# Retention and softmax-gated MLP on one core: from tile 20 the activation is transposed by DMA, with three more load buffers and new orders

## The chip, the cores and the metric

The kernel runs on one core of a Trainium2 chip. The core has a matrix engine (TensorE; PE in the tables, with PEld for its weight loads), a vector engine (DVE), a scalar engine (ACT), a general engine (POOL), and a queue engine (SP) that issues DMAs; all five run their own instruction lists and wait for each other by semaphores. The metric is the device time of one execution in microseconds.

## The reference

`q`, `k`, `v` are (8 batches, 8 heads, 576 positions, 64), float32. Retention is computed for each head, the heads are joined to rows of 512, and each of the 4608 rows goes through a two-layer MLP:

```python
scores = scale * np.matmul(q, k.transpose(0, 1, 3, 2))
gamma = 1.0 - 2.0 ** (-5.0 - np.arange(H, dtype=np.float32))
Dmat = np.where(rel >= 0, gamma[:, None, None] ** rel[None, :, :], 0.0)
x = np.matmul(scores * Dmat[None], v)            # then (B, S, H, D) as (4608, 512)
h = x @ w_in                                     # (4608, 1024)
e = np.exp(h - h_max)
sm = e / (np.sum(e, axis=-1, keepdims=True) + 1e-09)
solu = h * sm
mu = np.mean(solu, axis=-1, keepdims=True)
var = np.mean((solu - mu) ** 2, axis=-1, keepdims=True)
ln = (solu - mu) / np.sqrt(var + 1e-06) * g_ln
out = ln @ w_out                                 # (4608, 512)
```

## The kernel before

The work is cut twice into 36 pieces. A step `i` is half of the heads (four) of a window of 256 positions (or of the last 64 positions of four batches); two steps make a window, and a window gives two row tiles `t` of 128 rows for the MLP. Each piece of work has a name, a letter code with the number of its step or tile:

- `ldq`, `ldk`, `ldv` load a step's inputs (SP; L379, or four parts at L384), `sq`, `sk` scale and cast q and k to f16 by the decay factors, `cv` casts v (POOL, in the opening ACT or DVE).
- `T` transposes q and k on PE into PSUM (L429), `S` the scores (L508), `mask` multiplies them by the decay mask on DVE (L540), `V` scores times v (L472), `K` the state update, `I` the part that comes from the state, `st`, `sm`, `sc` the state's bookkeeping on DVE and POOL, `xe` the copy of the result to `xT` on ACT.
- `M1` is the first MLP product, eight matmuls into the one PSUM buffer `h` (L587); `ex` the exponential on ACT (L595); `so` the product h times e in f16, tile `solu` of 128x1024, on DVE (L610); `bnA`, `bnB` the row statistics on DVE (L616); `rs` the row's factor on POOL.
- `L` transposes `solu` on PE into PSUM, as 32 matmuls of 64x64 against the identity (L446); from then on `solu` is the left operand of `M2`, the second product (L660). `oe` scales its result on ACT, `out` stores it (SP).

From tile 4 the transposes of step `i` and of tile `i - 6` share one PSUM tile `tl` (two banks), and one ACT copy `TL` of 128x1024 takes both to an SBUF tile of the pool `ev` (eight buffers). The last tiles have copies of their own, `Le`. `M2` of tile `t` runs right behind `M1` of tile `t + 4`.

PSUM is full: `xy`, `s`, `h` with one buffer of two banks each and `tl` with two banks. `S` and the result of `M2` take turns in `s`. Raw inputs have five buffers for each of q, k and v; the weights' staging `wst` has five buffers of 4 KB a partition and is used only until the weights are cast, scaled and centred in the opening (`wi`, `wg`, `wc`).

The order on each engine is fixed beforehand: `plan()` lists the pieces with costs, dependencies and buffers, `order_ops()` runs through each engine's list and interleaves them; within an engine the list decides. Of that list the first and last parts are written out (`FIRST`, `LAST`), and the middle follows due times, a period per tile. The queue engine SP works through its list in order too: a DMA that has to wait holds those behind it. In the opening, where PE would idle, matmuls on zeros are put in (L846). At the end, a count of rows whose sums lie outside a safe range decides a branch (`cnt`, `cs`, `ci`; L853, L916); with this case's data it goes to the short way, which evicts and stores the last half tile.

Of the kernel before, what the change touches and what calls it, by code (L numbers as in the profile page):

```python
# [13 lines left out]
P = 128  # L14
# [3 lines left out]
for _b in range(0, B, 4):  # L18
# [9 lines left out]
    ldx=0.88, ldw=1.36, out=0.65,  # L28
# [8 lines left out]
    rawq=5, rawk=5, rawv=5, q16=3, k16=4, v16=4, ev=8, s=1, ret=2, xy=1, gg=6, gt=2, s160=4, s161=9, h=1,  # L37
    e=2, solu=4, osb=3, tl=1, tlx=2, tlT=1, tlL=1, wst=5,
# [3 lines left out]
FIRST = dict(  # L42
    PE=(
# [5 lines left out]
    ),  # L49
    ACT=(  # L50
# [4 lines left out]
    ),  # L55
    DVE=(
# [5 lines left out]
    ),  # L62
    POOL=(
# [4 lines left out]
    ),  # L68
    SP=(
# [35 lines left out]
def ev_T(i):  # L105
    return f"Te{i}" if i < NJ + 2 else f"TL{i - 2}"


def ev_L(t):
    return f"Le{t}" if t < NJ - 4 or t + 4 > NS - 3 else f"TL{t + 4}"  # L110
# [6 lines left out]
def wide(name):  # L117

    return name[0] == "T" and int(name[1:]) < NJ + 2 or name[0] == "L" and int(name[1:]) < NJ - 4


def plan():
    ops = []
    rank = {n: x - 1e4 for lst in FIRST.values() for x, n in enumerate(lst.split())}
    rank.update({n: x + 1e4 for lst in LAST.values() for x, n in enumerate(lst.split())})
# [835 lines left out]
```

## Time and profile before

| | |
|---|---|
| time, median of 3 runs | 213.56 us (212.74 to 213.57) |
| profiled execution, first to last instruction | 210.9 us |
| DMA | 42.66 MB, mean 202 GB/s |
| HBM read, written | 32.55 MB, 9.44 MB |
| instructions | 10171 |

The profile is of one execution. Its rows give, for a group of instructions, the line of the kernel, the engine, the operation, what is written from what with shapes, the count, then the busy time and the mean of one in ns, then the engine's idle time ahead of them with what ended it. Rows of the timeline begin with the start and the duration in us; neighbours of one kind are merged, and matmuls overlap, so the start of the next group tells more of a group's cost than its duration. Rows of the stage view give a window of time, its length, and the busy time of each engine in it.

### The profile page before, as it was taken

To read this page: it belongs to the slowest core of one execution; us is meant where nothing else is said; L and a number is where in the kernel's file an instruction comes from. 1 tells how busy PE (TensorE), PEld (TensorE's weight loads), DVE (VectorE), ACT (ScalarE), POOL (GpSimd) and SP (SyncE) were. 2 spreads that over 40 slices of the span, in tenths; PEclk is the share of its full clock that TensorE was granted. 3 is DMA by queue.
4 is the path that set the end of the run, shared out by engine and by line. 5 is a ranking of instruction groups with operands and counts; after the bars stand their busy time and mean duration, and the time that the engine had idled before them with its cause. 6 is when DMAs were issued, how large, how long until landed. Compare 5 with 4: busy or idle time off the path is not lost. (4 is left out here: it accounts for less than half of the span.)

```text
span 210.9 us, 10171 instructions
## 1 busy us (share of the span) xinstructions
PE 200.8 (95%) x4400; PEld 113.2 (54%) x4400; DVE 166.1 (79%) x279; ACT 141.7 (67%) x235; POOL 141.7 (67%) x240
## 2 busy tenths in 40 slices
PE   7986989999999999999999999999999999999992
PEld 2442654665566555555555555555666555554451
DVE  6565779997868898978898898889988998753760
ACT  2375787897666776776666777666767777573752
POOL 7434758999997975948787979797979792001110
PEclk9999999999999999999999999999999999999999
DMA  5999999999666559778999686776355222311224
GB/s 157 345 355 334 329 311 269 301 293 306 195 188 188 169 139 278 217 214 259 314 288 305 198 252 183 217 234 181 94 152 153 54 57 67 71 63 54 101 101 104
DMA packets 64814, 42.66 MB, mean 202 GB/s; under 512 B 3320, under 2 KB 58624, under 8 KB 64768
## 3 DMA queue, kind: packets, MB, share of 16 engines
q1 hardware_dynamic: 64528, 41.82, 68.4%
q8 instruction: 34, 0.56, 1.2%
q10 hardware_dynamic: 240, 0.18, 0.5%
q14 instruction: 12, 0.10, 0.2%
HBM read 32.55 MB, written 9.44 MB: 199 GB/s over the span
## 5 line engine op out<-in xcount | busy, mean ns | idle before, releaser
L587 PE MATMUL h_ps<-w_in,xT 128*128 128x512 f16 x288 | 68.5, 380 | 0.0
L660 PE MATMUL o_ps<-w2c,ev 128*128 128x512 f16 (+1 forms) x296 | 67.6, 373 | 0.0
L610 DVE TENSOR_TENSOR solu<-h_ps,e_sb 128x1024 f16<-128x1024 f32 x32 | 39.2, 1223 | 16.7 <-ACT e_sb L595 16.5
L595 ACT ACTIVATE e_sb<-h_ps 128x1024 f32<-128x1024 f32 x36 | 36.8, 1023 | 21.9 <-PE h_ps L587 20.4
L540 DVE TENSOR_TENSOR ret<-s_ps,masks 128x1024 f16<-128x1024 f32 x36 | 43.9, 1220 | 6.0 <-PE s_ps L508 5.4
L660 PEld LDWEIGHTS <-ev 128*128 128x128 f16 x296 | 28.7, 98 | 32.7
L616 DVE BATCH_NORM_STATS2 bs<-solu 128x6 f32<-128x512 f16 x64 | 43.6, 685 | 0.9
L587 PEld LDWEIGHTS <-xT 128*128 128x128 f16 x288 | 25.3, 98 | 29.1 <-ACT xT L576 0.8
L394 POOL TENSOR_TENSOR q<-rawq,small 128x512 f16<-128x512 f32 x34 | 35.4, 1042 | 7.3 <-DMA rawq<-in_q_dram 5.9
L669 ACT ACTIVATE o_sb<-o_ps,rs 128x512 f32<-128x512 f32 (+1 forms) x37 | 25.0, 676 | 21.8 <-PE o_ps L660 10.4
L394 POOL TENSOR_TENSOR k<-rawk,small 128x512 f16<-128x512 f32 x34 | 35.4, 1042 | 6.0 <-DMA rawk<-in_k_dram 5.9
L457 ACT COPY ev<-tl 128x1024 f32<-128x1024 f32 (+1 forms) x32 | 29.7, 932 | 4.7 <-PE tl L429 4.2
L576 ACT CAST xT<-xy 128x512 f16<-128x512 f32 x36 | 26.7, 742 | 3.0 <-PE xy L472 2.9
L571 POOL CAST sbd<-gg 64x256 f16<-64x256 f32 x64 | 25.4, 397 | 3.0
L562 POOL TENSOR_TENSOR gg<-gt,small 128x128 f32<-128x128 f32 x32 | 13.1, 409 | 16.9 <-DVE gt L557 16.5
L648 POOL TENSOR_TENSOR w<-mv,w 128x2 f32<-128x2 f32 x16 | 3.1, 194 | 27.8 <-ACT w L633 13.9
L399 POOL CAST v<-rawv 128x512 f16<-128x512 f32 x28 | 17.1, 609 | 0.2
L508 PE MATMUL s_ps<-ev 64*64 64x128 f16 x576 | 14.8, 218 | 0.3
L472 PE MATMUL xy<-ret,v 64*64 64x128 f16 x576 | 14.7, 217 | 0.0
L472 PEld LDWEIGHTS <-sbd 128*128 128x128 f16 x128 | 9.3, 98 | 9.3 <-issue 1.1
L446 PE MATMUL tl<-ident,solu 64*64 64x64 f16 x1024 | 14.2, 195 | 0.0
L846 PE MATMUL tl<-zeros 128*128 128x512 f16 x41 | 12.7, 445 | 1.3 <-DVE zeros L802 1.3
(71 smaller groups left out, 214.6 us busy)
## 6 DMA issues: line engine op xcount, KB each, us to landing
rawq<-in_q_dram SPq DMA_DIRECT2D x32, 256.0 KB, 5.1
rawk<-in_k_dram SPq DMA_DIRECT2D x32, 256.0 KB, 5.3
rawv<-in_v_dram SPq DMA_DIRECT2D x32, 256.0 KB, 5.1
out_dram<-o_sb SPq DMA_DIRECT2D x26, 256.0 KB, 3.1
out_dram<-o_sb SPq DMA_DIRECT2D x19, 128.0 KB, 2.3
wst<-in_moe_w_in_dram SPq DMA_DIRECT2D x4, 512.0 KB, 6.8
wst<-in_moe_w_out_dram SPq DMA_DIRECT2D x4, 512.0 KB, 7.1
rawq<-in_q_dram SPq DMA_DIRECT2D x16, 64.0 KB, 2.4
```

The lines of the kernel that those rows point to most:

```text
L394: eng.tensor_tensor(out=t.rearrange("p j h d -> p h j d"), in0=st[i]["r" + nm], in1=g, op=ALU.mult)
L457: nc.scalar.copy(out=t[:, lo:hi].rearrange("p x (r w) -> p r x w", r=2), in_=tls[n].rearrange("p r x w -> p (r x w)").bitcast(FP).rearrang ...
L472: nc.tensor.matmul(start=(c, e) not in begun, stop=False, skip_group_check=True, **kw)
L540: nc.vector.tensor_tensor(out=d["ret"].rearrange("p e h j q -> p (e h) (j q)"), in0=d["s"].rearrange("p e h j q -> p (e h) (j q)"), in1=ma ...
L571: nc.gpsimd.tensor_copy(out=t[ee[e], :, :, ee[e]], in_=st[i]["gg"][ee[e]])
L576: nc.scalar.copy(out=xT[:, 2 * w : 2 * w + 2, 2 * hf : 2 * hf + 2].rearrange("p c h (q j) -> p c h j q", j=2), in_=xys[i][:, :, 0:256].rea ...
L587: nc.tensor.matmul(out=h_ps[:, hh], lhsT=xT[:, t, dc], rhs=w_in16[:, dc, hh], start=(dc == 0), stop=(dc == 3),)
L595: nc.scalar.activation(out=d["e"], in_=d["h"], func=ACT.Exp, accum_out=se[:, t : t + 1])
L610: nc.vector.tensor_tensor(out=d["solu"], in0=d["h"], in1=d["e"], op=ALU.mult)
L616: nc.vector.bn_stats(out=d["bs"][:, half], in_=d["solu"][:, half * 512 : half * 512 + 512])
L660: nc.tensor.matmul(out=o, lhsT=d["ev"][:, d["lo"] + c], rhs=w2c16[:, c, mm], start=(c == 0), stop=(c == 7))
L669: nc.scalar.activation(out=d["osb"][:, mm], in_=d["o", half], func=ACT.Copy, scale=ws[t // 2]["rs"][:, t % 2 : t % 2 + 1])
```

## The change

Three things are changed.

1. For tiles 20 to 33 (`LX`) the 32 matmuls of `L` are gone. In their place SP issues one DMA transpose (`lx`, function `ln_dma`) from `solu` to an `ev` buffer of its own. Steps 26 and later no longer share `tl` with a tile; ACT copies their half alone (`Te` in place of `TL`). The code also has a like way for q and k (`TX`), and two banks `o2` for `M2` (`OT`); both are off here.
2. Once the weights are done, the space of `wst` is given to a pool `bis` with three more raw buffers for each of q, k and v. They are used by steps 18 to 20, 26 to 28, 34 and 35 (`extra`).
3. The order of every engine is now written out in full (`ORDER`), in place of `FIRST`, `LAST` and the due times between. In the opening the first steps, the loads and the fillers (45 before, 40 after) stand in another order; in the middle V, T, K and S of neighbouring steps change places; loads are spread otherwise among the stores; at the end `M2_33` stands ahead of `M1_35`, and `cnt` behind `so35`.

```diff
-    rawq=5, rawk=5, rawv=5, q16=3, k16=4, v16=4, ev=8, s=1, ret=2, xy=1, gg=6, gt=2, s160=4, s161=9, h=1,
-    e=2, solu=4, osb=3, tl=1, tlx=2, tlT=1, tlL=1, wst=5,
+    rawq=5, rawk=5, rawv=5, bisq=3, bisk=3, bisv=3, q16=3, k16=4, v16=4, ev=8, s=1, ret=2, xy=1, gg=6, gt=2, s160=4, s161=9, h=1,
+    e=2, solu=4, osb=3, o2=2, tl=1, tlx=2, tlT=1, tlL=1, wst=5,
...
+LX = (20, 21, 22, 23, 24, 25, 26, 27, 28, 29, 30, 31, 32, 33)
+TX = ()
+R0 = 13
+OT = 99
...
-FIRST = dict(
+ORDER = dict(
     PE=(
...
-        "V14 S15 M1_12 M2_8 I15 L11 T17 V15 S16 M1_13 M2_9 I16 L12 T18 V16 K18 S17 M1_14"
+        "T0 K0 S0 T1 K1 S1 I0 V0 I1 V1 G M1_0 K2 T2 S2 T3 K3 M1_1 S3 I2 V2 L0 I3 V3 L1 T4 K4 M1_2 S4 K6 WM K5 M1_3 T5 K7  "
...
+        "M2_15 I22 L18 V22 K24 T24 S23 M1_20 M2_16 I23 L19 T25 V23 K25 S24 M1_21 M2_17 I24 T26 V24 K26 S25 M1_22 M2_18  "
+        "I25 V25 T27 K27 S26 M1_23 M2_19 I26 V26 T28 K28 S27 M1_24 M2_20 I27 V27 K29 T29 S28 M1_25 M2_21 I28 T30 V28 K30  "
...
+        "I32 V32 T34 S33 M1_30 M2_26 I33 V33 T35 S34 M1_31 M2_27 I34 V34 S35 M1_32 I35 V35 M2_28 M1_33 M2_29 M2_31 M1_34  "
+        "M2_30 M2_33 M1_35 L34 M2_32 L35 cs M2_34 M2_35 M3"
...
     SP=(
-        "ldq0 ldk0 ldv0 ldv1 ldq1 ldk1 lwi1 lwi2 lwi0 lwi3 ldk2 ldv2 ldq2 ldk3 ldq3 ldv3 lwo4 lwo0 ldk4 ldq4 "
-        "ldv4 lwo6 ldk6 lwo2 ldv6 ldk5 ldv5 ldk7 ldq5 ldv7 ldq6 ldk8 ldq7 ldq8 ldk9 ldv8 ldq9 ldq10 ldv9 "
...
+        "ldk0 ldq0 ldv0 ldq1 ldk1 ldv1 lwi1 lwi2 lwi0 lwi3 ldq2 ldv2 ldk2 ldk3 ldq3 ldv3 lwo4 lwo0 ldk4 ldq4 ldv4 lwo6  "
+        "lwo2 ldk6 ldv6 ldk5 ldv5 ldq5 ldv7 ldk7 ldk8 ldq6 ldq7 ldq9 ldk9 ldq8 ldq11 ldv8 ldv9 ldv11 ldk10 ldv10 ldv16  "
+        "ldq10 ldv12 ldv20 ldq13 ldk11 ldq12 ldk13 ldk14 ldk19 ldq15 ldk12 ldk18 ldk15 ldq14 out0 ldq18 ldv14 ldk16 out2  "
...
+        "out16 lx20 ldk30 ldk31 ldk35 ldv31 lx21 out17 out18 lx22 ldk33 out19 lx23 ldv30 ldq30 ldv32 ldk34 lx24 out20  "
+        "ldq35 ldk32 lx25 ldq34 out21 lx26 out22 ldv34 lx27 ldv35 out23 out25 lx28 out24 lx31 out26 lx29 out28 lx32  "
+        "out27 lx30 out29 lx33 out30 out31 out32 out33 out34 out35"
...
 def ev_L(t):
-    return f"Le{t}" if t < NJ - 4 or t + 4 > NS - 3 else f"TL{t + 4}"
+    return f"lx{t}" if t in LX else f"Le{t}" if t < NJ - 4 or t + 6 >= NS or t + 6 in TX else f"TL{t + 4}"
+
+
+def extra(i):
+    return i >= R0 and (i - R0) % 8 >= 5
...
+        if t in LX:
+            op(f"lx{t}", "SP", "lx", [f"so{t}"], (m + 2, 0.1), [("ev", [f"M2_{t}"])], DUR["ltx"])
...
-        st[i]["r" + nm] = t = pools["raw"].tile([P, 4, 2, D], FP, tag=nm, name="raw" + nm)
+        if extra(i) and "bis" not in pools:
+            loads_w.close()
+            pool("bis", CAP["bisq"])
+        st[i]["r" + nm] = t = pools["bis" if extra(i) else "raw"].tile([P, 4, 2, D], FP, tag=nm, name="raw" + nm)
...
+    def blocks():
+        t = pools["ev"].tile([P, 16, 64], FP, tag="ev", name="ev")
+        return t.rearrange("p x w -> p (x w)").bitcast(F16).rearrange("p (x w) -> p x w", w=P)[:, 0:8]
...
+    def ln_dma(t):
+        tk[t]["lo"] = 0
+        tk[t]["ev"] = x = blocks()
+        nc.sync.dma_start_transpose(out=x, in_=tk[t]["solu"])
...
+        elif k_ == "lx":
+            ln_dma(x)
```

The rest of the diff moves pools (`wst` is opened last, so that its space can be given back), gives the general path of the branch a buffer of its own, and carries the parts that are off.

More of the change, by code (lines that the diff above doesn't have):

```diff
@@ L136, in plan @@
         n = i - 2
+        tt = f"tx{i}" if i in TX else f"T{i}"
         for x, (nm, cs) in enumerate((("q", "sq"), ("k", "sk"), ("v", "cv"))):
-            op(f"ld{nm}{i}", "SP", 0.47 if full else 1.8, [], (i - 3 - CAP["rawq"], 1.5 + x), [("raw" + nm, [f"{cs}{i}"])], DUR["ldx"])
-        op(f"sq{i}", "POOL", dict(POOL="sq", DVE="sqD"), [f"ldq{i}"], (i - 3, 0.5), [("q16", [f"T{i}"])])
-        op(f"sk{i}", "POOL", dict(POOL="sk", DVE="sqD"), [f"ldk{i}"], (i - 3, 1.55), [("k16", [f"T{i}", f"K{i}" if full else ""])])
+            op(f"ld{nm}{i}", "SP", 0.47 if full else 1.8, [f"wc{y}" for y in range(8)] if extra(i) else [],
+               (i - 3 - CAP["rawq"], 1.5 + x), [(("bis" if extra(i) else "raw") + nm, [f"{cs}{i}"])], DUR["ldx"])
+        op(f"sq{i}", "POOL", dict(POOL="sq", DVE="sqD"), [f"ldq{i}"], (i - 3, 0.5), [("q16", [tt])])
+        op(f"sk{i}", "POOL", dict(POOL="sk", DVE="sqD"), [f"ldk{i}"], (i - 3, 1.55), [("k16", [tt, f"K{i}" if full else ""])])
         op(f"cv{i}", "POOL", dict(POOL="cv", DVE="cvD", ACT="cvA"), [f"ldv{i}"], (i - 3, 2.6), [("v16", [f"V{i}", f"K{i}" if full else ""])])
@@ L183, in plan @@
         early = t < NJ - 4
[L184 to L188 removed]
+        if t in LX:
+            op(f"lx{t}", "SP", "lx", [f"so{t}"], (m + 2, 0.1), [("ev", [f"M2_{t}"])], DUR["ltx"])
+        lasts = [x for x in range(NT) if NJ - 4 <= x < OT and ev_L(x)[:2] == "Le"]
+        after = [f"Te{NJ + 1}", f"Le{NJ - 5}"] if t == NJ - 4 else []
+        if t in lasts:
+            after += [f"Le{t - 2}" if t - 2 in lasts else ev_T(max(i for i in range(NS) if i not in TX))]
+        if t not in LX:
+            op(f"L{t}", "PE", "Lw" if wide(f"L{t}") else "L", [f"so{t}"] + after, (m + 2, 0.1),
+               [("tlL" if early else "o2" if t >= OT else "tl" if jn else "tlx", [ev_L(t)])])
+        if ev_L(t)[:2] == "Le":
             op(f"Le{t}", "ACT", "Le", [f"L{t}"], (m + 2, 0.95), [("ev", [f"M2_{t}", "M3" if t == NT - 1 else ""])])
@@ L191, in plan @@
         need = [ev_L(t)] + [f"wc{x}" for x in range(8)] + ["cs" if t == NT - 2 else ""]
-        op(f"M2_{t}", "PE", "M2h" if end else "M2", need, (t + LAG, 3.1), [("h" if end else "xy" if late(t) and t % 2 else "s", [f"oe{t}"])])
+        if t == OT:
+            need += [ev_T(min(TX) - 1), ev_L(max(x for x in range(NT) if x not in LX and x < min(LX)))]
+        op(f"M2_{t}", "PE", "M2h" if end else "M2", need, (t + LAG, 3.1), [(home(t), [f"oe{t}"])])
         op(f"oe{t}", "ACT", "oeh" if end else "oe", [f"M2_{t}", f"rs{w}"], (t + LAG + 1, 0.1), [("osb", [f"out{t}"])])
@@ L223, in parts @@
 def parts(name):
-    if name[:2] == "lw":
+    if name[:2] in ("lw", "lx"):
         return 1
+    if name[:2] == "tx":
+        return 2
     n = int(name[3:])
@@ L339 @@
     pool("raw", CAP["rawq"])
-    for name in ("q16", "k16", "v16", "ev", "ret", "gg", "gt", "e", "solu", "osb", "wst"):
+    for name in ("q16", "k16", "v16", "ev", "ret", "gg", "gt", "e", "solu", "osb"):
         pool(name, CAP[name])
@@ L400, in cast_v, with bank @@
         st[i]["v16"] = t
+    def bank():
+        if "o2" not in pools:
+            banks_2.close()
+            pool("o2", CAP["o2"], space=PS)
+        return pools["o2"].tile([P, 512], FP, tag="o2", name="o_ps")
     def tl_of(n):
@@ L654, in mm2 @@
         d = tk[t]
-        nm = "xy" if half or late(t) and t % 2 else "s"
-        nm = "h" if t == NT - 1 and not half else nm
+        nm = "xy" if half else home(t)
         mm = slice(256 * half, 256 * half + (256 if t == NT - 1 else DM))
-        d["o", half] = o = pools[nm].tile([P, 2, 512], FP, tag=nm, name="o_ps")[:, 0, 0 : mm.stop - mm.start]
+        o = bank() if nm == "o2" else pools[nm].tile([P, 2, 512], FP, tag=nm, name="o_ps")[:, 0]
+        d["o", half] = o = o[:, 0 : mm.stop - mm.start]
         for c in range(8):
@@ L867 @@
                 emit(o)
+    if "bis" not in pools:
+        loads_w.close()
+    pool("gu", 1)
     def general(t):
```

84 lines of the change are left out of this document (40 added, 44 removed), and 55 rows, old and new, of tables (ACT, DVE, PE, POOL).

## Prediction

> **What bounds the kernel now.** I read the page's totals first, then the stages, then one period of the steady stretch, then the end.
>
> ```profile
> span 210.9 us, 10171 instructions
> PE 200.8 (95%) x4400; PEld 113.2 (54%) x4400; DVE 166.1 (79%) x279; ACT 141.7 (67%) x235; POOL 141.7 (67%) x240
> ...
> 0.00:50.00 50.00, 44.59 (x678) 24.43 (x679) 36.54 (x74) 34.57 (x61) 35.08 (x62) 1.00 1.06 299
> 50.00:110.00 60.00, 59.57 (x1547) 34.65 (x1546) 51.58 (x82) 41.60 (x67) 47.83 (x80) 1.00 0.77 226
> 110.00:170.00 60.00, 60.00 (x1577) 34.66 (x1575) 54.11 (x86) 42.04 (x67) 51.05 (x86) 1.00 0.64 184
> 170.00:200.00 30.00, 30.00 (x535) 15.84 (x534) 20.68 (x31) 19.14 (x33) 6.81 (x13) 1.00 0.23 65
> 200.00:210.90 10.90, 6.65 (x70) 3.65 (x68) 3.17 (x8) 4.37 (x10) 0.93 (x3) 0.98 0.33 102
> ```
>
> The stage rows give the window, its length, the busy time of PE, PEld, DVE, ACT and POOL, then TensorE's granted clock and the DMA share. From 50 to 200 us PE is busy 149.6 of 150 us at a clock of 1.00, so what is taken off PE there comes off the time, until another limit is met. DVE stands second (54.1 of 60 us). Before 50 us PE has 5.4 us of gaps, and the DMA engines are full (share 1.06). Here is one period, with the end of it:
>
> ```profile
> 133.85 1.90 PE L587 MATMUL h_ps<-w_in,xT 128*128 128x512 f16 x8
> ...
> 135.79 1.02 ACT L595 ACTIVATE e_sb<-h_ps 128x1024 f32<-128x1024 f32 x1 [0.67 <-PE h_ps L587]
> ...
> 136.94 1.22 DVE L610 TENSOR_TENSOR solu<-h_ps,e_sb 128x1024 f16<-128x1024 f32 x1 [0.31 <-ACT e_sb L595]
> ...
> 137.31 0.39 PE L472 MATMUL xy<-ev,sbd 128*128 128x128 f16 x4
> 137.63 0.45 PE L446 MATMUL tl<-ident,solu 64*64 64x64 f16 x32
> 137.91 0.30 PE L429 MATMUL tl<-ident,q 64*64 64x64 f16 x16
> ...
> 138.85 1.47 PE L587 MATMUL h_ps<-w_in,xT 128*128 128x512 f16 x6
> ```
>
> PE does I (137.31), L (the solu transpose, 137.63), T (137.91) and so on back to back. L shows 0.45 us busy, but the next group starts 0.28 us after it: matmuls overlap, and the pitch of 0.28 is what L costs. All L together in the table of groups, and below it PE's first M2, which I take as the end of the opening:
>
> ```profile
> L446 PE MATMUL tl<-ident,solu 64*64 64x64 f16 x1024 | 14.2, 195 | 0.0
> ...
> 45.25 1.89 PE L660 MATMUL o_ps<-w2c,ev 128*128 128x512 f16 x8
> ```
>
> Those 1024 matmuls are the L of tiles 4 to 35, 32 each. Two loops lie close underneath the period. The h loop: M1 starts at 133.85, its exponential at 135.79, the product that frees the single h buffer ends at 136.94 + 1.22 = 138.16, so the next M1 could have started some 0.1 us later, 4.40 us after this one; it starts at 138.85. The DVE loop:
>
> ```profile
> 122.16 1.22 DVE L610 TENSOR_TENSOR solu<-h_ps,e_sb 128x1024 f16<-128x1024 f32 x1 [0.31 <-ACT e_sb L595]
> ...
> 171.49 1.22 DVE L610 TENSOR_TENSOR solu<-h_ps,e_sb 128x1024 f16<-128x1024 f32 x1 [0.29 <-ACT e_sb L595]
> ```
>
> Ten periods (tiles 19 to 29) take 49.33 us, 4.93 each, and DVE idles 0.31 in each, so DVE alone could do 4.62.
>
> **L leaves PE for tiles 20 to 33.** Fourteen groups of 32 go. L20 to L30 (from 132.63 us on) stand in the saturated chain: 11 x 0.28 = 3.08 us. The new period, 4.93 - 0.28 = 4.65, still lies above DVE's 4.62 and the h loop's 4.40. With 0.03 us of room DVE will not keep exact step; I charge 0.3 us over the eleven (bounds 0, and 0.1 a period, 1.1). The last three L stand where other things rule:
>
> ```profile
> 182.91 1.90 PE L587 MATMUL h_ps<-w_in,xT 128*128 128x512 f16 x8
> ...
> 187.31 1.89 PE L587 MATMUL h_ps<-w_in,xT 128*128 128x512 f16 x8
> ...
> 192.49 1.89 PE L587 MATMUL h_ps<-w_in,xT 128*128 128x512 f16 x8
> ...
> 197.22 1.90 PE L587 MATMUL h_ps<-w_in,xT 128*128 128x512 f16 x8
> ...
> 200.65 1.22 DVE L610 TENSOR_TENSOR solu<-h_ps,e_sb 128x1024 f16<-128x1024 f32 x1
> ...
> 202.50 0.45 PE L446 MATMUL tl<-ident,solu 64*64 64x64 f16 x32
> ...
> 206.75 0.47 ACT L669 ACTIVATE o_sb<-o_ps,rs 128x256 f32<-128x256 f32 x1 [0.41 <-PEq L916]
> ```
>
> These are M1_32, M1_33, M1_34, M1_35, so35, L35 and the last eviction. M1_32 to M1_33 is already 4.40, the h loop, so L31 saves nothing. M1_33 to M1_34 (5.18: one M1 and two M2) holds no L. From M1_34 to L35 it was 10.01 us. The new order puts two M2 between M1_34 and M1_35 (5.18) and one M2 and L34 after it; then L35 waits for so35, 4.31 + 0.1 after M1_35: 9.6. After L35 PE has the same work, but the last `rstd` hangs on so35 as before, and the count for the branch now stands between so35 and the statistics, so I keep only 0.2 of the 0.4 us. Sum so far: -3.08 + 0.3 - 0.2 = -3.0.
>
> **The transposes on the DMA.** The old trace holds no DMA transpose. Each moves 128x1024 f16, 256 KB, from SBUF to SBUF. The nearest rows:
>
> ```profile
> rawq<-in_q_dram SPq DMA_DIRECT2D x32, 256.0 KB, 5.1
> ...
> out_dram<-o_sb SPq DMA_DIRECT2D x26, 256.0 KB, 3.1
> ...
> 140.78 0.37 SPq L379 DMA_DIRECT2D rawv<-in_v_dram  x1
> ...
> 159.55 14.34 SPq L680 DMA_DIRECT2D out_dram<-o_sb  x9
> ...
> SPq L680 <- ACT o_sb L669: 53.8, 24, 5.3
> ```
>
> The last figure of the first two rows is the time from issue to landing. The same 256 KB takes 3.1 us as a store, most of them issued when the queues are quiet, and 5.1 as a load, many of them in the crowded opening. The transposes run when the DMA share is 0.64 and then 0.23, so I take 3.1 and keep 5.1 as the other bound. For tiles 20 to 28, `solu` is finished 4.31 us after M1_t starts, and M2_t runs after M1_(t+4), itself 1.73: 4 x 4.65 + 1.73 - 4.31 = 16 us, hidden at either bound. Tile 33 is tight. so33 ends when M1_34 starts, and PE runs M1_34 and M2_30 (1.73 + 1.74) and then wants M2_33: 3.47 us. At 3.1 it waits for nothing; at 5.1 M2_33, and M1_35 behind it, start 1.6 us late. I take 0, bounds 0 and +1.6.
>
> The transposes issue on SP, and each adds a wait there: lx_t waits for so_t, with loads and stores queued behind. Of those, q30 is nearest: behind lx23, which is released as M1_24 starts, it issues some 1.1 us later, lands 5.1 later at worst, and POOL scales it in 1.04: 7.3 us, against T30 8.4 us after M1_24 (4.65, 1.73, 1.74, and 0.32 for I). So 1.1 us are left, more if it lands sooner. An issue costs 0.37 us (rawv row), and SP sits waiting for evictions (53.8 us in all): hidden, unless a transpose holds SP or the DMA engines far longer.
>
> **What comes free, and what is only reordered.**
>
> ```profile
> L457 ACT COPY ev<-tl 128x1024 f32<-128x1024 f32 x26 | 26.3, 1013 | 4.7 <-PE tl L429 4.2
> L595 ACT ACTIVATE e_sb<-h_ps 128x1024 f32<-128x1024 f32 x36 | 36.8, 1023 | 21.9 <-PE h_ps L587 20.4 <-DVE bs L616 1.4
> ...
> L457 ACT COPY ev<-tl 128x512 f32<-128x512 f32 x6 | 3.4, 582 | 0.0
> ...
> POOL q L394 <- DMA rawq<-in_q_dram: 5.9, 2, 4.6
> POOL k L394 <- DMA rawk<-in_k_dram: 5.9, 6, 2.7
> ...
> 15.59 2.05 PE L587 MATMUL h_ps<-w_in,xT 128*128 128x512 f16 x8
> ...
> 35.96 0.40 PE L419 MATMUL tl<-ident,q 128*128 128x128 f16 x4 [0.38 <-POOL q L394]
> ```
>
> ACT copies half as much for tiles 26 to 33 and on (1.01 to 0.58 us each), but its exponential waits for M1 (20.4 us in all), not for that copy: 0. A tile now takes two `ev` buffers of the eight, one for some 16 us and one for some two periods, 5 or 6 in flight: 0.
>
> The three extra load buffers serve tiles 18 to 20, 26 to 28, 34 and 35. POOL's waits for loads are 11.8 us in 8 places, all of them in the opening, before the weights have left their staging: 0. The new opening drops five filler matmuls and lets q0's scale go ahead of the copy that waits for the first matmul. The first M1 (15.59) needs all four `w_in` loads, and as many bytes are loaded before them as before, so it keeps its place. Later `q5` is loaded and scaled before `k7`, which is worth the 0.38 us of PE's wait at 35.96 and perhaps 1 us more; in return 512 KB of `w_out` go ahead of `k6`, which at 299 GB/s is 1.7 us later. These differ in sign and I cannot tell which one lasts: 0, bounds -1.5 and +1.5. Between 50 and 130 us the swaps of V, T, K and S hold the same matmuls, and PE has no gap to give: 0.
>
> **Sum.** -3.0 us. Against the profile's own time that is a span of 210.9 - 3.0 = 207.9. The median of the runs shown, 213.56, lies 2.66 above that span (what lies around the span, taken as unchanged), so the time is 210.6.
>
> **The rivals.** (a) The freed PE time is eaten by DVE. For it: 0.03 us of room, and the loop from mask over M2 and the next M1 to the next product is as tight. Against it: DVE keeps its order and its 0.31 us of idle time in every period. At 0.15 us lost a period: 1.65 instead of 0.3, 211.9.
>
> (b) Landing takes 5.1 us. Then M2_33 waits 1.6; if q30 behind them also lands 1.6 later than the 5.1 I gave it, T30 waits 1.6 - 1.1 = 0.5: 212.7. For it: the loads' median; against it: the late, quiet DMA.
>
> (c) Slower: the transposes leave one at a time. From the end of so20 to the point where PE wants M2_33 are 64.2 us (eleven periods at 4.65, then 4.40, 5.18 and 3.47). Fourteen transposes at T us each, not overlapping, cost 14 T - 64.2 beyond that: from T = 4.59 they set the pace, and from 4.88 the kernel is slower than before by over 0.5% (3.0 + 1.07 us). If the landing time of a load, 5.1 us, were such a serial time, it would be 71.4 - 64.2 = 7.2 us more: 217.8. For it: nothing in the trace excludes it, as the operation is new. Against it: loads issue every 0.5 to 0.6 us and land in 5.1, so plain transfers overlap. The Trainium skill speaks for this one: "VectorE: DVE Perf Modes", section "The three transpose paths", gives the DMA crossbar 1309 ns for one 128x128 block and advises TensorE where PSUM will do as the target. Eight blocks one after the other would be an estimated 10.5 us, and 14 x 10.5 - 64.2 = 83 us more, some 294. No row of the old trace can test that figure; the 0.28 us that PE takes for the same eight blocks shows why it would matter.
>
> (d) The opening decides: 1.5 us worse gives 212.1, 1.5 better 209.1.
>
> **How the numbers follow.** Chances: forecast 0.48 (210.6), (a) 0.10 (211.9), (b) 0.13 (212.7), (c) 0.20 (217.8, with a long tail), (d) 0.09, mostly on the good side. Half a per cent of 213.56 is 1.07 us, about what a measurement of this kernel can tell from no change, so "same" is 212.5 to 214.6. Faster: forecast, (a), most of (d): 0.66. Same: (b) and the rest: 0.14. Slower: (c): 0.20. The likeliest case's own range is 209.1 to 212.1. The range has to reach further: down to the good opening and an exact 0.28 a period, 208.8; up through (b) with a bad opening (214.2) into the lower part of (c), where T is just under 5 us: 216.
>
> **What would show it.** Right: the steady period after 130 us at 4.65 to 4.70, PE still without gaps there, the transposes landing in about 3 us, L446 down from 1024 to 576 matmuls, M1_34 some 3 us earlier. Wrong: PE waits at M2 on `ev` from the DMA, at T on POOL (late q), or the period stays above 4.8 with DVE busy throughout (a); SP issues of the transposes longer than 2 us or landings that grow from tile to tile (c); a first M2 more than 1 us away from its old 45.25 us (d).

## The result, and the profile after

The changed kernel takes 222.42 us (median of 4 executions, 218.46 to 226.24) against 213.44 for the kernel before on the same chip (4 executions, 212.74 to 213.57). The ratio is 1.031, 95% interval 1.023 to 1.040: slower, where 210.6 us was forecast. It leaves out the two slow executions, of which one (223.37 us) is profiled below, and compares the other two (218.46 and 221.47 us, 5.0 and 8.0 above the 213.44) with the kernel before. The span of the profiled execution is 221.6 us, 10.7 more than before.

The page of the changed kernel, with a row of its groups and one of its DMA issues (last figure: us from issue to landing):

```profile
span 221.6 us, 9250 instructions
...
PE 202.7 (91%) x3947; PEld 112.2 (51%) x3947; DVE 163.8 (74%) x279; ACT 135.0 (61%) x231; POOL 141.1 (64%) x240
...
PEclk9999999999999889999999999999999967999997
...
L492 PE MATMUL tl<-ident,solu 64*64 64x64 f16 x576 | 8.0, 195 | 0.3 <-DVE solu L671 0.3
...
ev<-solu SPq DMA_TRANSPOSE x14, 3.2
```

The view of the line that issues the transposes gives their time on SP (minimum, median, maximum in ns, first and last start), and who waited for them and for how long:

```profile
L521 SPq DMA_TRANSPOSE ev<-solu x14: 1237/1309/2905, 133.9 to 202.9; - x14
...
  PEld L721: 1.1, 2
  PE o_ps L721: 0.3, 1
```

L is down from 1024 to 576 matmuls as planned, and a transpose lands in 3.2 us, as taken; PE waited for its result 0.3 us in all (its weight loads 1.1). But PE, busy 95% of the span before, is at 91%, and its clock has two dips. And SP is held 1.3 us by each transpose, where a plain load held it 0.37. The stages, cut as in the prediction, without the last:

```profile
0.00:50.00 50.00, 42.83 (x667) 23.86 (x668) 36.06 (x75) 33.93 (x60) 33.28 (x60) 1.00 1.01 292
50.00:110.00 60.00, 58.29 (x1427) 33.46 (x1426) 48.24 (x76) 39.41 (x64) 47.61 (x76) 0.97 0.87 254
110.00:170.00 60.00, 59.78 (x1355) 33.84 (x1353) 51.35 (x85) 39.60 (x68) 49.37 (x86) 1.00 0.77 179
170.00:200.00 30.00, 25.69 (x361) 13.08 (x360) 18.36 (x27) 13.74 (x25) 8.21 (x15) 0.89 0.50 97
```

The two dips have the same form. The first, at 73 us, stands 60 us ahead of the first transpose:

```profile
63.53 2.84 SPq L421 DMA_DIRECT2D rawq<-in_q_dram  x4
66.47 1.80 SPq L421 DMA_DIRECT2D rawk<-in_k_dram  x4
68.32 0.43 SPq L416 DMA_DIRECT2D rawv<-in_v_dram  x1
...
73.20 0.61 POOL L436 CAST v<-rawv 128x512 f16<-128x512 f32 x1 [3.56 <-DMA rawv<-in_v_dram]
...
74.67 0.28 PE L533 MATMUL xy<-ev,sbd 128*128 128x128 f16 x2 [1.38 <-POOL sbd L632]
...
77.10 3.01 PE L648 MATMUL h_ps<-w_in,xT 128*128 128x512 f16 x8
```

The load of v15 is issued at 68.32, behind the eight parts of q16 and k17, which are needed later. POOL's list is in order: `cv15` waits 3.56 us, and behind it stand the state cast for which PE waits, and the scale of k. Then M1 takes 3.01 us, not 1.90. The second, at 175 us:

```profile
164.05 1.30 SPq L521 DMA_TRANSPOSE ev<-solu  x1
165.44 1.19 SPq L741 DMA_DIRECT2D out_dram<-o_sb  x2
166.68 3.18 SPq L421 DMA_DIRECT2D rawv<-in_v_dram  x4
169.96 1.27 SPq L521 DMA_TRANSPOSE ev<-solu  x1
171.33 2.93 SPq L421 DMA_DIRECT2D rawv<-in_v_dram  x4
...
176.00 1.17 POOL L436 CAST v<-rawv 128x512 f16<-128x512 f32 x2 [5.54 <-DMA rawv<-in_v_dram]
...
179.01 0.39 PE L533 MATMUL xy<-ev,sbd 128*128 128x128 f16 x2 [3.69 <-POOL sbd L632]
...
180.76 3.60 PE L648 MATMUL h_ps<-w_in,xT 128*128 128x512 f16 x8
```

From 164 to 178 us SP's timeline has no pause of over 0.15 us (it waits 0.4 us for evictions there, in the kernel before 11.1); v34 and v35 come out of its list at 166.68 and 171.33 behind the transposes of tiles 26 and 27, and POOL waits 5.54 us for them. The start of M1 in PE's timeline tells where the time goes (us; the third column has the difference to before since the row above it):

```
M1 of tile   before   after    lost since the row above
5             48.44    49.58    +1.14 (opening)
9             68.83    69.66    -0.31
11            78.63    83.14    +3.68
29           168.41   171.58    -1.34
31           178.16   187.74    +6.41
35           197.22   207.76    +0.96
end          210.9    221.6     +0.16
```

In this execution the two dips are 10.1 of the 10.7 us.

### The profile page after: what moved, and what is told of

The parts are those of the page before. It is cut to its first block, busy times and chain, and to the rows that moved or that the text cites. A ratio compares the mean times of both kernels' runs of the same rounds, so it can differ in the third digit from the quotient of the medians.

```text
span 221.6 us, 9250 instructions
## 1 busy us (share of the span) xinstructions
PE 202.7 (91%) x3947; PEld 112.2 (51%) x3947; DVE 163.8 (74%) x279; ACT 135.0 (61%) x231; POOL 141.1 (64%) x240
## 4 chain that ended last, share of the span: by engine, by line
PE 52%; DMA 21%; SPq 11%; DVE 4%; POOL 4%; issue 3%; ACT 2%; POOLq 0%; ACTq 0%; DVEq 0%
PE h_ps L648 19%; PE o_ps L721 19%; DMA rawv<-in_v_dram 9%; SPq L416 7%; PE xy L533 6%; DMA rawq<-in_q_dram 5%; PE s_ps L569 3%; DMA out_dram<-o_sb 3%; PE tl L473 3%; DMA rawk<-in_k_dram 3%; SPq L421 2%; DMA ev<-solu 2%; DVE ret L601 2%; PE tl L492 1%; POOL q L431 1%
## 5 line engine op out<-in xcount | busy, mean ns | idle before, releaser
L648 PE MATMUL h_ps<-w_in,xT 128*128 128x512 f16 x288 | 71.2, 392 | 0.4 <-DVE gln L845 0.4
L677 DVE BATCH_NORM_STATS2 bs<-solu 128x6 f32<-128x512 f16 x64 | 42.9, 680 | 0.2
L648 PEld LDWEIGHTS <-xT 128*128 128x128 f16 x288 | 26.2, 100 | 31.7 <-issue 3.9
L431 POOL TENSOR_TENSOR k<-rawk,small 128x512 f16<-128x512 f32 x34 | 35.9, 1057 | 8.5 <-DMA rawk<-in_k_dram 7.8
L637 ACT CAST xT<-xy 128x512 f16<-128x512 f32 x36 | 26.6, 738 | 10.2 <-PE xy L533 10.1
L503 ACT COPY ev<-tl 128x1024 f32<-128x1024 f32 (+1 forms) x28 | 23.3, 830 | 5.1 <-PE tl L473 5.1
L533 PE MATMUL xy<-ev,sbd 128*128 128x128 f16 (+1 forms) x128 | 12.5, 214 | 5.5 <-POOL sbd L632 5.1
L569 PE MATMUL s_ps<-ev 64*64 64x128 f16 x576 | 15.4, 224 | 0.9 <-ACT o_sb L730 0.2
L533 PE MATMUL xy<-ret,v 64*64 64x128 f16 x576 | 15.2, 225 | 0.1
L711 POOL TENSOR_TENSOR rs<-w,small 128x2 f32<-128x2 f32 x18 | 12.5, 692 | 1.4
```

Source lines behind the costliest of these rows:

```text
L431: eng.tensor_tensor(out=t.rearrange("p j h d -> p h j d"), in0=st[i]["r" + nm], in1=g, op=ALU.mult)
L503: nc.scalar.copy(out=t[:, lo:hi].rearrange("p x (r w) -> p r x w", r=2), in_=tls[n].rearrange("p r x w -> p (r x w)").bitcast(FP).rearrang ...
L533: nc.tensor.matmul(start=(c, e) not in begun, stop=False, skip_group_check=True, **kw)
L637: nc.scalar.copy(out=xT[:, 2 * w : 2 * w + 2, 2 * hf : 2 * hf + 2].rearrange("p c h (q j) -> p c h j q", j=2), in_=xys[i][:, :, 0:256].rea ...
L648: nc.tensor.matmul(out=h_ps[:, hh], lhsT=xT[:, t, dc], rhs=w_in16[:, dc, hh], start=(dc == 0), stop=(dc == 3),)
L677: nc.vector.bn_stats(out=d["bs"][:, half], in_=d["solu"][:, half * 512 : half * 512 + 512])
```

## The experiments

Theory A: the new orders put single loads late in SP's list, POOL and then PE stand still, and TensorE's clock falls behind the gap; the transposes matter only because they make SP's list longer. Theory B: the transposes are the cause, by SP's time or by their traffic. SP's entries below are named as in the order lists. Lines of the experiments' kernels are six higher than those of the changed kernel, some more behind an added line. All times are medians; "before" is between 212.8 and 213.0 in each group of runs. The starts of M1 and the span's end, for all that are spoken of:

```
M1 of tile          5      9      11     20      21      27      31      35     end    time
before            48.44  68.83  78.63  123.96  128.85  158.63  178.16  197.22  210.9   213.44
before again      49.39  69.77  79.58  124.59  129.48  159.26  178.78  197.85  211.5   213.23
after             49.58  69.66  83.14  127.86  133.02  161.97  187.74  207.76  221.6   222.42
new orders alone  49.49  70.13  81.87  126.59  133.47  163.50  183.19  202.30  215.9   217.40
old orders + lx   49.38  69.76  79.57  124.40  129.29  157.96  177.07  196.09  209.8   212.95
v34, v35 first    48.84  69.80  81.18  126.44  131.66  160.33  187.10  207.09  220.2   221.94
and v15 first     48.95  69.76  80.08  124.79  129.97  158.64  185.21  205.19  218.3   221.48
all late loads    49.13  69.87  80.31  126.53  132.81  161.48  182.09  202.67  215.8   218.58
loads and lx      48.76  70.39  80.50  125.21  131.21  159.93  180.11  199.63  213.0   213.77
four parts apart  50.32  70.71  80.52  125.97  130.86  159.53  178.64  197.67  211.4   212.32
```

**The new orders without the transposes.**

```diff
-LX = (20, 21, ..., 33)
+LX = ()
```

with `L20` to `L33` ahead of `T26` to `T35` and in the tail as before, and `TL`, `Le` back in ACT's list.

> The new orders and the three extra buffers, with L20 to L33 back on TensorE and no DMA transposes. Theory A (the new orders make single loads late; TensorE then stands still, and its granted clock falls behind the gap; the transposes only make SP's list longer at the end): the gaps at about 45 and 73 us are still there (M1_11 at 83 us, where before has 78.6), the one at 175 us is gone or small, since SP has 14 x 1.3 = 18 us less to do; time 217 to 219. Theory B (the transposes, by SP's time and the DMA share, cost what was lost): M1_11 at 78 to 79 and a time of 212 to 214, as before.

Measured: 217.40 us, ratio 1.0185 (1.0125 to 1.0244). The gap at 73 us is there (M1_9 to M1_11 11.74 us, before 9.80), the one at 175 us is not. So the new orders lose 4 us without any transpose: B alone falls. Of what is lost here the changed kernel's profile has only the gap at 73 us; a further hole of 1.9 us before M1_21 had not been expected, and the changed kernel's profile does not show it. The gap itself:

```profile
75.00 0.28 PE L539 MATMUL xy<-ev,sbd 128*128 128x128 f16 x2 [1.24 <-POOL sbd L638]
...
76.12 0.32 PE L479 MATMUL tl<-ident,k 64*64 64x64 f16 x16 [0.33 <-POOL k L437]
...
76.94 1.90 PE L654 MATMUL h_ps<-w_in,xT 128*128 128x512 f16 x8
```

The waits are nearly those of the changed kernel (1.38 and 0.33), but M1 behind them takes its usual 1.90 us, not 3.01.

**The old orders with the transposes.** FIRST, the due times and LAST of the kernel before, written out; `L20` to `L33` removed; in SP's list

```diff
-... out16 ldq31 ldk31 ldv31 out17 ldq32 ...
+... out16 lx20 ldq31 ldk31 ldv31 out17 lx21 ldq32 ...
```

and so on, `lx33` behind `out29`. (The opening has 53 fillers here, where the kernel before has 45; M1_5 starts as in the second profile of before.)

> The orders of before, no extra buffers, but tiles 20 to 33 transposed by DMA: L20 to L33 leave TensorE, and each transpose stands behind out(t-4) in SP's list. Theory A: no gap at 45 and 73 us, periods of 4.65 to 4.7 behind 130 us because T still stands ahead of V and not of K, 209.5 to 211.5. Theory B: a gap of 4 us or more behind 165 us, 215 to 219, because 1.3 us of SP for each transpose makes the loads of the last steps late in any order.

Measured: 212.95 us, ratio 1.0013 (0.9981 to 1.0046). No gap, so B alone falls again: fourteen transposes that hold SP for as long (median 1.32 us) cost nothing in the old list. Nor do they reach A's 209.5 to 211.5, though the periods in this profile, of the shortest of the ten executions, are 4.75 and 4.80 where before had 4.89 and 5.00.

**The last v loads ahead.**

```diff
-lx24 out20 ldq35 ldk32 lx25 ldq34 out21 lx26 out22 ldv34 lx27 ldv35 out23
+ldv34 ldv35 lx24 out20 ldq35 ldk32 lx25 ldq34 out21 lx26 out22 lx27 out23
```

> The changed kernel, but the loads of v34 and v35 (4 parts each) stand ahead of the transpose of tile 24 in SP's list, not behind those of 26 and 27. Theory A: cv34 and cv35 no longer wait on POOL, the 6.4 us lost between M1_29 and M1_31 shrink to under 1.5, the gaps at 45 and 73 us stay; 215 to 217. Theory B: the gap stays or moves, as the same number of transposes is still ahead of the same number of loads in all; 220 to 223.

Measured: 221.94 us, a miss for A as put, and within B's 220 to 223. The gap moved two tiles forward. From the timeline of SP and POOL in this kernel:

```profile
152.19 5.29 SPq L427 DMA_DIRECT2D rawv<-in_v_dram  x8
...
161.43 1.07 SPq L422 DMA_DIRECT2D rawk<-in_k_dram  x1
...
165.29 1.04 POOL L437 TENSOR_TENSOR k<-rawk,small 128x512 f16<-128x512 f32 x1 [6.96 <-DMA rawk<-in_k_dram]
```

The eight parts moved ahead hold SP 5.29 us, and now k32 behind them is late, by more. So no single load is the cause: behind 144 us the list has no room. This B would say too; what tells the two apart is whether the loads can be placed so that the gap goes with all the transposes in place.

**And v15 ahead.**

```diff
-out2 ldv13 ldv18 out1 ldq16 ldk17 ldv15 ldq19
+out2 ldv13 ldv18 ldv15 out1 ldq16 ldk17 ldq19
```

> As the run before it, and the load of v15 stands ahead of the store of tile 1, not behind the 4-part loads of q16 and k17. Theory A: also the gap at 73 us is gone (M1_9 to M1_11 in 10 us, not 13.5), 211.5 to 213.5. Theory B: 220 to 223. If the time comes down by less than 3 us against the run before it, v15 was not the last that was late there.

Measured: 221.48 us, again in B's range for the time. At the place it was made for, it did what A says: M1_9 to M1_11 takes 10.32 us (11.38 in the run before it, 13.48 in the changed kernel). The time hardly fell, because the late gap stayed (17.0 us for M1_27 to M1_29, two periods).

**All late loads ahead.** On top of that, every load of steps 30 to 35 as early as its buffer is free:

```diff
-lx20 ldk30 ldk31 ldk35 ldv31 lx21 out17 out18 lx22 ldk33 out19 lx23 ldv30 ldq30 ldv32 ldk34 ldv34 ldv35 lx24 out20 ldq35 ldk32 lx25 ldq34 out21 ...
+lx20 ldk30 ldk31 ldv31 lx21 out17 ldk33 ldk32 ldk35 ldk34 ldv30 ldq30 ldv32 out18 lx22 ldv34 ldv35 out19 ldq34 ldq35 lx23 out20 lx24 lx25 out21 ...
```

> As the run with v15 and the last v loads first, but now every load of the last six half-windows stands in SP's list as early as its buffer comes free, ahead of the transposes of tiles 23 to 33, as many transposes as before. Theory A (each single load that is moved ahead makes another one late, because SP's list behind 144 us is full: 14 transposes of 1.3 us and 24 parts of loads; the loads must all be ahead of the transposes): no gap of over 1 us behind 130 us, M1_23 to M1_33 in 47.5 us, 211 to 213.5. Theory B (the transposes slow the loads' landing itself by their packets): a gap stays at 165 to 180 us, 216 or more.

Measured: 218.58 us (215.27 to 219.76). M1_27 to M1_31 fell from 26.57 (the run before it) to 20.61 us: the late gap is all but gone with fourteen transposes in place. The time misses A's 211 to 213.5 and lies in B's range (216 or more), but not by B's gap: what was left are holes of 0.8 to 1.5 us at M1_14, M1_21, M1_28 and M1_35. At the one before M1_28 and at the last M2 waited for a transpose, which now stood behind the loads:

```profile
164.71 1.90 PE L727 MATMUL o_ps<-w2c,ev 128*128 128x512 f16 x8 [1.32 <-DMA ev<-solu]
...
200.93 1.90 PE L727 MATMUL o_ps<-w2c,ev 128*128 128x512 f16 x8 [0.65 <-DMA ev<-solu]
```

**The extra buffers on top of the old orders** (`R0 = 13` in the second run).

> The old orders with the transposes as in the second run, and the three extra buffers for loads on top. Theory A: within 0.6 us of that run (212.4 to 213.5), because no load was late there by the time of its use. Rival: the loads issued earlier meet the stores and the stages of the opening, 213.5 to 215.

Measured: 212.88 us, ratio 1.0011 (0.9979 to 1.0043): on the old orders the buffers do nothing. Its profile shows one place where this order loses some of what the transposes gain:

```profile
164.99 0.38 SPq L747 DMA_DIRECT2D out_dram<-o_sb  x1
...
167.37 0.69 ACT L736 ACTIVATE o_sb<-o_ps,rs 128x512 f32<-128x512 f32 x1 [1.15 <-PE tl L479]
...
168.11 0.42 PE L575 MATMUL s_ps<-ev 64*64 64x128 f16 x16 [0.47 <-ACT o_sb L736]
```

The store of tile 21 is issued at 164.99, behind the twelve parts of q35, k35 and v35; there are three output buffers, so the eviction of tile 24 has to wait for that store to land (the releaser that the row names, PE's transpose, writes another tile; the store is worked out from the count of buffers). It starts at 167.37, and the scores S wait for it: M1_29 comes 0.5 us late.

**What sets the period now.** In the second run's profile:

```profile
147.31 0.69 ACT L736 ACTIVATE o_sb<-o_ps,rs 128x512 f32<-128x512 f32 x1 [0.66 <-POOL w L715]
...
148.05 0.42 PE L575 MATMUL s_ps<-ev 64*64 64x128 f16 x16
```

M2's result and the scores take turns in the PSUM buffer `s`. S starts 0.74 us behind the start of the eviction `oe`, that is 0.05 behind its end, and so it does in every period from M1_22 on (0.73 or 0.74); the periods of 4.75 and 4.80 differ by when `oe` starts. To test this, `oe` was lengthened and shortened for tiles 17 to 27. First M2 and `oe` in two halves of 256 columns, hoping that the first half would be evicted early:

```diff
+        return (slice(0, 256), slice(256, 512)) if 17 <= t < 28 else (slice(None),)
...
+        for x in halves(t):
+            for c in range(8):
...
-                out=o, lhsT=d["ev"][:, d["lo"] + c], rhs=w2c16[:, c, mm], start=(c == 0), stop=(c == 7)
+                    out=o[:, x], lhsT=d["ev"][:, d["lo"] + c], rhs=w2c16[:, c, mm][:, x], start=(c == 0), stop=(c == 7)
```

> The old orders with the transposes as in the second run, and M2 and the eviction oe of tiles 17 to 27 in two halves of 256 columns. Theory S (with L gone the scores S wait until oe has left the PSUM bank that o_ps and s_ps share, S starts 0.74 us behind the start of oe in each step, and this round of M1, M2, oe, S is 4.75 to 4.80 long, where the sum of TensorE's work is 4.65): S starts 0.1 us or more earlier against M2, periods of 4.65 to 4.70 between M1_22 and M1_32, 0.8 to 1.3 us less than the second run: 211.5 to 212.3. Rival (VectorE's chain sets the 4.75 to 4.80): periods unchanged, 212.6 to 213.4.

Measured: 216.71 us, ratio 1.0167 (1.0114 to 1.0220), periods of 4.92 and 4.97: a miss for the number, as the eviction did not come earlier. Both halves ran after the whole of M2, and together they are longer:

```profile
151.37 0.84 ACT L741 ACTIVATE o_sb<-o_ps,rs 128x256 f32<-128x256 f32 x2 [0.68 <-POOL w L715]
...
152.26 0.42 PE L575 MATMUL s_ps<-ev 64*64 64x128 f16 x16
```

An `oe` 0.15 us longer makes every period 0.17 longer, S again 0.05 us behind its end. (The opening of this profile is some 3 us later than the others', which its edit does not explain.) Then the other way:

```diff
+        x = slice(0, 256) if 17 <= t < 28 else mm
...
-            out=d["osb"][:, mm], in_=d["o", half], func=ACT.Copy, ...
+            out=d["osb"][:, x], in_=d["o", half][:, 0 : x.stop - x.start], func=ACT.Copy, ...
...
+        if x.stop - x.start < mm.stop - mm.start:
+            nc.scalar.copy(out=d["osb"][:, 256:512], in_=zeros[:, 256:512])
```

This kernel leaves out columns 256 to 511 of the result of these tiles, so it serves as a test of the wait only.

> The old orders with the transposes, as in the second run; in the tiles 17 to 27 the eviction oe reads only columns 0 to 255 of o_ps out of PSUM, and ScalarE fills the other 256 columns of the output from zeros in SBUF, so these columns are left out. Theory S (S waits for the end of oe, since o_ps and s_ps share a bank): the periods of 4.80 become 4.65 or less and those of 4.75 stay (there TensorE's own work is 4.75), M1_22 to M1_32 takes 47.0 to 47.3 us where the second run has 47.78. Rival (VectorE or the round of M1, exp, so): 47.7 or more.

Measured: 212.29 us, ratio 0.9963 (0.9929 to 0.9997); M1_22 to M1_32 takes 47.04 us against 47.78, with one eviction late in it, which waits 1.29 us for a store (the profile names it, as worked out above) and makes M1_29 some 0.5 us late. The other periods are 4.62 and 4.74:

```profile
143.01 0.47 ACT L737 ACTIVATE o_sb<-o_ps,rs 128x256 f32<-128x256 f32 x1 [0.61 <-PE o_ps L727]
143.38 0.39 ACT L742 CAST o_sb<-zeros 128x256 f32<-128x256 f16 x1
143.63 0.40 PE L575 MATMUL s_ps<-ev 64*64 64x128 f16 x16
143.96 1.90 PE L654 MATMUL h_ps<-w_in,xT 128*128 128x512 f16 x8
```

So both the 4.75 and the 4.80 are the round of M1, M2, `oe` and S (only the 4.80 was expected to fall), and with that round shorter PE's own work of 4.62 to 4.74 appears: the 4.89 and 5.00 of before less some 0.27. DVE and the h loop, which this run leaves as they were, did not set the 4.75 and 4.80.

**The kernel before again.**

> The kernel before, unchanged, for a second profile of it: how much of the opening (M1_5 at 48.4 us in the first one) differs from one execution to the next. Within 1 us: then the opening of the changed kernel (M1_5 at 49.6) lost nothing that can be told from this.

Measured: 213.23 us; M1_5 at 49.39. Its opening differs by 0.95 us from that of the first profile, so the 1.14 us of the changed kernel's opening are no loss that can be told.

**Loads one store earlier, and the second run again.** With the old orders, the transposes and the buffers: loads of steps 26 to 33 one store earlier, the 4-part loads of steps 34 and 35 one at a time behind `lx21` to `lx26`.

> The old orders with the transposes and the extra buffers; SP's list changed alone: the loads of steps 26 to 33 one store earlier, and the six 4-part loads of steps 34 and 35 one at a time behind the transposes of tiles 21 to 26 instead of three in a row. Theory A (the second run gives its gain of 1.7 us back in most executions, because stores and transposes stand behind 8 us of 4-part loads in SP's list and oe waits for its buffer): no hiccup over 0.3 us between M1_22 and M1_33, 211.0 to 212.2, faster than before by 0.4 to 0.8 per cent. Rival (the second run's executions are longer for another reason, such as the DMA share): 212.5 to 213.5.

> The second run's kernel unchanged, for another profile of it: its first profile was the shortest of ten executions. If the theory above is right, this one shows 0.5 to 1.5 us lost between M1_25 and M1_33 at an eviction that waits for a store, or the loss stands in the opening.

Measured: 212.95 us, ratio 0.9996 (0.9970 to 1.0023), the rival's number, and 211.75 (one execution) for the second run's kernel. The first has no hiccup behind M1_22, as A says, but lost 0.8 and 0.6 us at M1_15 and M1_18, where its loads now are. The second shows no late eviction in its profile, so it does not tell where the longer executions of that kernel lose.

**The changed kernel, repaired.** From the run with all late loads ahead, still in SP's list alone: `ldk26` ahead of `out12`, the 4-part loads of v34, v35, q34 and q35 one at a time between transposes and stores, and the last transposes in the order of their tiles:

```diff
-out18 lx22 ldv34 ldv35 out19 ldq34 ldq35 lx23 out20 lx24 lx25 out21 lx26
+out18 lx22 ldv34 out19 lx23 ldv35 out20 lx24 ldq34 lx25 out21 ldq35 lx26
```

> As the run with all late loads ahead (its SP list), and besides the load of k26 ahead of the store of tile 12 (it stood behind the store of tile 14, for which SP waited 10 us), the 4-part loads of v34, v35, q34, q35 one at a time between transposes and stores, and the transposes of tiles 24 to 33 one place further ahead, since M2 waited for three of them. Theory A (what is left of the loss is more of the same: things that stand too late in SP's list): the 6.3 us steps at M1_20 to M1_21 and M1_27 to M1_28 and the 6.0 at the end fall to 5.2 or less, M1_35 at 197.5 to 199.5, 212.5 to 215.5. Theory C (TensorE's lower granted clock behind any gap, or the new orders of the other engines, hold the rest): 216 or more with the same steps.

Measured: 213.77 us (211.97 to 216.89), ratio 1.0015 (0.9981 to 1.0049). The whole loss is gone by SP's list alone, with PE, ACT, DVE and POOL in the new orders and the transposes and buffers in place: neither the new orders of the engines nor the transposes, by their time on SP or by their traffic, cost it by themselves. The step before M1_28 fell from 6.3 to 4.8 us, the last from 6.0 to 5.2; a new hole of 0.8 us stands before M1_29, where S waits for an eviction. The one before M1_21 stayed (6.0, from 6.3): my reading that k26 caused it was wrong. There PE stops in the middle of L:

```profile
128.88 0.38 PE L498 MATMUL tl<-ident,solu 64*64 64x64 f16 x22
...
130.16 0.28 PE L498 MATMUL tl<-ident,solu 64*64 64x64 f16 x10 [0.91 <-issue]
```

No wait that the profile shows ended it; the cause stays open.

**Four parts one at a time.** The old orders, transposes and buffers; against the second run only this:

```diff
-lx23 ldq34 ldk34 ldv34 out20 lx24 ldq35 ldk35 ldv35 out21 lx25 out22 lx26
+lx21 ldq34 ... lx22 ldk34 ... lx23 ldv34 out20 lx24 ldq35 out21 lx25 ldk35 out22 lx26 ldv35
```

> The old orders with the transposes and extra buffers; SP's list as in the second run except that the six 4-part loads of steps 34 and 35 stand one at a time behind the transposes of tiles 21 to 26. Unlike the run with loads one store earlier, nothing is moved into the stretch of 95 to 120 us where the DMA share is over 0.9. Theory A: that run's 0.8 and 0.6 us at M1_15 and M1_18 are gone and no step behind M1_22 is over 4.85: 211.3 to 212.3, faster than before by 0.4 to 0.8 per cent. Rival: 212.6 to 213.4, no difference, as the two runs with the old orders and the transposes had it.

Measured: 212.32 us (211.46 to 213.12), ratio 0.9977 (0.9953 to 1.0001). From M1_22 to M1_33 no step is over 4.81, and M1_15 is in step again, but 0.8 us at M1_18 stayed. This has the lowest median of the complete versions with more than one execution, 6 to 9 us under the 218.46 and 221.47 us of the changed kernel; against the kernel before its interval just holds no difference, so that it is faster is likely but not shown. Why the old orders with the transposes do not turn the 1.5 us of their shorter periods into time in most executions is settled only in part.

## Why the prediction was wrong

**The failed step** is the one on SP: "An issue costs 0.37 us (rawv row), and SP sits waiting for evictions (53.8 us in all): hidden, unless a transpose holds SP or the DMA engines far longer." The condition at its end was the case, and the sum put nothing down for it: a transpose holds SP 1.31 us (median), 3.5 times the 0.37, fourteen of them some 18 us. The 53.8 us of waiting were no reserve either: they lie behind entries that wait, and in an in-order list the loads behind those wait too; ahead of the late gap none of it was left (0.4 us from 164 to 178 us, where the kernel before has 11.1). I followed one load, q30, past the transposes; k32, v34 and v35, which the new list puts behind more of them, were not followed. In the profiled execution this costs 6.4 us, part of it by the clock (below), and it takes both the transposes and the new list: neither the transposes in the old orders nor the new orders without them have that gap, and the repaired list, with both, does not have it either.

**The step beside it** also failed: "the swaps of V, T, K and S hold the same matmuls, and PE has no gap to give: 0." Where the two orders can be compared, the swaps do cost nothing: M1_11 to M1_20 takes 44.72 us in the changed kernel and 44.83 in the second run, and the periods around M1_24 are 4.75 and 4.80 in both. (The hole before M1_21 appears only with the new orders; its cause is open.) But the same lists spread the loads otherwise among the stores, and I priced only PE's part. v15 behind eight parts of later loads made a gap where PE had none: 3.7 us in the profiled execution, 1.9 in the run with the new orders alone.

**L's matmuls:** the mechanism was right, the size was not. I charged 2.8 us for eleven periods (0.28 each less 0.3 for DVE). From M1_21 to M1_32 the second run takes 52.53 us against 54.05 in the second profile of before: 1.5 us gained. The term that was mis-sized is the new period, 4.65: the round over the shared PSUM buffer holds the periods at 4.75 and 4.80, and the half-eviction run shows 4.62 and 4.74 without it. In the kernel before, the same two rows:

```profile
147.45 0.69 ACT L669 ACTIVATE o_sb<-o_ps,rs 128x512 f32<-128x512 f32 x1 [0.66 <-POOL w L648]
...
148.29 0.41 PE L508 MATMUL s_ps<-ev 64*64 64x128 f16 x16
```

S starts 0.84 us behind the start of `oe` here, and 0.89, 0.95 or 1.00 in the periods beside it: 0.10 to 0.26 above the 0.74 at which it has to wait. That margin, less than the 0.28 to be taken out, could have been read. DVE was not as near as the prediction had it: its 0.31 us are only the idle time ahead of `so`, while its own stage row has DVE idle 5.89 of 60 us, 0.48 a period; in the half-eviction run DVE still idles 0.18 us or more ahead of `so`. So (a) was not what held the period.

**The landing** was right in the changed kernel (3.1 taken, 3.2 measured; the second run's median is 4.0, still hidden), and so were the buffers (0, on the old orders) and the opening (0 within 1.5); ACT's halves (0) were not tried apart. That tile 33 was in time was in part luck: `so33` ended 1.37 us ahead of M1_34, where the prediction had it end with it, but its transpose was issued 1.65 us after that, behind other entries of SP. M1_34 to M1_35 is 5.18, as said. The 0.2 us at the end are not to be seen: from M1_34 to the end it was 18.4 us before, 19.0 after and 18.6 in the repaired kernel.

**The rivals.** The result is on the side of (c) but not by its mechanism: the transposes do not leave one at a time at 4.6 us or more (in the second run's profile some are issued 2.7 us apart), and PE waited 0.3 us for them. The figure of the Trainium skill that spoke for it ("VectorE: DVE Perf Modes", "The three transpose paths", 1309 ns a block) does not carry over to eight blocks in one DMA: 3.2 us were measured, not 10.5. Another page has it nearer: "Advanced Engine Details and Errata", section "X-Bar Transpose (TRN2)", says that such DMAs are as fast as regular ones; here 3.2 us stand beside 3.1 for a store of as many bytes in the kernel before.

**The clock** made both gaps of the profiled execution dearer. Around the first dip, in windows of 1 us (the columns as in the stages):

```profile
74.00:75.00 1.00, 0.33 (x15) 0.23 (x19) 0.57 (x1) 0.01 (x1) 0.86 (x3) 1.00 0.34 90
75.00:76.00 1.00, 0.67 (x69) 0.56 (x69) 0.00 (x0) 0.00 (x0) 1.00 (x2) 0.99 1.00 312
76.00:77.00 1.00, 1.00 (x63) 0.93 (x48) 0.00 (x0) 0.84 (x1) 1.00 (x2) 0.50 1.00 336
77.00:78.00 1.00, 1.00 (x11) 0.35 (x4) 0.78 (x1) 0.91 (x3) 0.88 (x3) 0.50 1.07 281
78.00:79.00 1.00, 1.00 (x4) 0.39 (x3) 0.97 (x4) 0.00 (x0) 0.93 (x1) 0.50 1.06 301
79.00:80.00 1.00, 1.00 (x5) 0.39 (x4) 0.77 (x2) 0.00 (x0) 0.92 (x4) 0.80 0.92 271
```

TensorE goes on at half clock from 76 to past 79 us. That is about 3.4 us at half speed, 1.7 us of work, beside the 1.7 us of waiting (1.38 and 0.33) that came before it. The run with the new orders alone bears this out: up to here its lists are the same, it waits 1.24 and 0.33 us at the same places, its clock stays at 1.00, and M1_9 to M1_11 takes 11.74 us, 1.7 less than the 13.48 of the changed kernel. At the second dip the clock is at half for about 6.8 us:

```profile
178.00:180.00 2.00, 0.98 (x34) 0.79 (x38) 0.00 (x0) 0.00 (x0) 1.86 (x4) 0.59 0.94 185
...
184.00:186.00 2.00, 2.00 (x8) 0.78 (x7) 0.46 (x1) 1.11 (x2) 0.09 (x1) 0.70 0.00 0
```

By the mean clocks of these rows it falls at some 178.4 us and is back at some 185.2; PE works in all but 0.6 us of that, so an estimated 3.1 us are lost. Of the 10.1 us of the two dips nearly half is then the clock's. The executions of this kernel differ in it: by time they took 218.46, 221.47, 223.37 and 226.24 us, at mean granted clocks of 0.993, 0.985, 0.972 and 0.972.

## What to carry to other kernels

Where one engine issues all DMAs in order, price a new DMA by how long it holds that engine (here 1.3 us, not 0.37), and then follow every load that stands behind it to its first use; idle time of that engine that is spent waiting for an earlier entry is no reserve. When work leaves the bounding engine, look for the next round that closes over a shared buffer: S started 0.10 to 0.26 us later than `oe` would have let it, in a period that was to lose 0.28. Move long multi-part loads apart from each other, so that stores and short loads can pass between them.

## What was not expected of the hardware

- One DMA transpose of 128x1024 f16 within SBUF holds the issuing engine for 1.24 to 2.9 us, median 1.31, and lands in 3.1 to 5.5 us (the changed kernel). Four loads of 64 KB each hold it 1.8 to 3.3 us together.
- The transposes nearly fill the DMA engines, which the prediction took to be quiet: from 134 to 182 us the DMA share is 0.46 in the kernel before and 0.96 in the second run, at 124 and 192 GB/s.
- How long PE waits does not tell whether TensorE's clock falls: behind waits of 1.38 and 0.33 us close together it went to 0.50 in the changed kernel, behind waits of 1.24 and 0.33 at the same place in the run with the new orders alone it stayed at 1.00, and so it did behind that run's hole of 1.79 us before M1_21 and the 0.91 in the repaired kernel. "TensorE: Matmul & The Clock Gate" of the Trainium skill, section "What's actually happening", has the clock halved after an idle window of about 3.4 us. The time at half clock agrees; the waiting that led to it was shorter here.
- PE stopped 0.91, 1.20 and 1.79 us inside one group of L, at the same step in three kernels with the new orders (before M1_21), with no wait that the profile shows.
